# Taking a turned softmax block to its place through DRAM instead of by small transfers inside the chip

## The chip, the cores and the metric

The kernel runs on one core of one Trainium2 chip. The metric is the device time of one execution in microseconds (us), as the median of several executions. Profiled executions give the rows that are shown; their times are read from the start of the profiled span.

## The reference, cut to what matters

```python
B, H, S, Ns, D = (8, 8, 512, 32, 64)          # x: B,H,S,D   state: B,H,Ns,D
scores  = softmax(scale * x @ state.T)        # over the 32 states
xread   = scores @ state
scores2 = softmax(scale * state @ x.T)        # over the 512 rows of x: the state softmax
sread   = scores2 @ x
z = concatenate([xread, sread], axis=2)       # B,H,544,64 -> 4352 rows of 512
h = z @ w_in                                  # 512 -> 2048
out = (h * tanh(softplus(h))) @ w_out         # 2048 -> 512
```

All of it is float32. The change touches only the way from `scores2` to `sread`.

## The kernel before, in words

The eight batches are worked off one after another. `state @ w_in` is formed for each batch and head first (tiles `swp`, split into a rounded high part `swh` and a rest `swl`), so that the first large product (tiles `ph`, function `gemm1`) runs straight from the attention weights `ah` and `al`, the high part and the rest of `at`. Mish turns `ph` into `gu`, sums of its parts (`sums`) and their high and low parts (`gh`, `gl`) feed the second large product (tiles `acc`, function `products`), whose results leave through `o`. After the `xread` rows of all batches come the `sread` rows of all of them (key "s").

The attention of batch b+1 is spread over the steps of batch b. For batches 3 to 7 the function `pieces` gives its vector work in small portions, and a table says at which step each comes. The order there is: `e1` (the scores turned, their maximum, the difference), both exponentials, `soft2_t` (lines 376 to 389, which the change rewrites), the sums and the division of `e1`, then `at` (`e1` turned back), `ah` by ScalarE and `al` by VectorE. TensorE reads the result of `soft2_t`, the tile `e2T`, in `sread`, at the head of the visit `sw0` of the batch (step 6 of the batch before); the same visit forms the batch's first `swp`, and ScalarE and VectorE make `swh` and `swl` from it.

Two things order this work. TensorE's instructions have the order in which they are written from start to end, and VectorE's and ScalarE's too, but for a stretch after the first batch (while `dve.on` and `act.on` are false, about 90 to 158 us), where a planner that simulates the engines puts them in order. SyncE's queue, which issues almost all transfers, is ordered by that planner throughout. A helper at line 93 records the engines' instructions, so nearly all rows name line 93.

Buffers matter too. The tiles `e1`, `e2b` (named `turned` in the code) and `at` share a tag with two buffers. `at` is made from `e1`, so it takes the buffer of `e2b`, and has to wait until nothing reads `e2b` any more:

```python
def temp(name):
    return pool.tile([P, 2, S], F32, tag="t", name=name)     # pool has bufs=2
```

`e2T` lies in the only buffer of the tag "sc", where the exponentials of the scores were. For the first batch both have places in another tile, and its transfers show in the profile as `scs<-e2b`.

Of the kernel before, what the change touches and what calls it, by code (L numbers as in the profile page):

```python
# [9 lines left out]
F32 = mybir.dt.float32  # L10
# [7 lines left out]
P = 128  # L18
B, H, S, NS, D = 8, 8, 512, 32, 64
DM, DF = 512, 2048  # L20
T = S + NS
NC = H // 2
NT = S // P
# [77 lines left out]
def state_attention_mish_kernel(ctx, tc, x_turned, x, state_wide, state, w_in, w_out, out):  # L101

    nc = tc.nc
# [22 lines left out]
    def temp(name):  # L126
        return pool.tile([P, 2, S], F32, tag="t", name=name)
# [8 lines left out]
    dram = ctx.enter_context(tc.tile_pool(name="dram", bufs=1, space=bass.MemoryType.DRAM))  # L136
# [192 lines left out]
    def flat2(a):  # L329
        return a.rearrange("p u s -> p (u s)")  # L330
# [4 lines left out]
    def attention(b):  # L335
# [26 lines left out]
        soft = {}  # L362
# [13 lines left out]
        def soft2_t():  # L376
            dve.tensor_scalar_add(soft["sm"], soft["sm"], 1e-9)
            dve.reciprocal(soft["rs"], soft["sm"])
            turned = flat2(temp(f"e2b_{b}"))
            dve.transpose(  # L380
                turned.rearrange("p (s q n) -> p q s n", s=4, q=8),
                soft["sc"].rearrange("p u (g s t) -> p (u g) s t", s=4, g=4))
            place = soft.pop("e2T") if b == 0 else pool.tile([P, 2, S], F32, tag="sc", name=f"e2T_{b}", bufs=1)
            e2T = soft["e2T"] = flat2(place).rearrange("p (c u t n) -> p c u t n", c=NC, u=2, t=NT)
            for c in range(NC):
                for s in range(4):
                    nc.sync.dma_start(  # L387
                        e2T[s * NS:(s + 1) * NS, c].rearrange("t u g n -> t (u g n)"),
                        turned[c * NS:(c + 1) * NS, s * 2 * P:(s + 1) * 2 * P])

        def soft1_t():
            e1 = soft["e1"] = temp(f"e1_{b}")
# [37 lines left out]
        def softs():  # L430
            whole(soft1_t())
            soft2_m()
            soft1_x()
            with behind("exp"):
                soft2_x()
            whole(soft1_n())
            soft2_t()

        def pieces():
# [14 lines left out]
            with behind("exp"):  # L454
                soft2_x()
            yield
            soft2_t()
            yield
            dve.tensor_reduce(sums, g, AX.X, ALU.add)
# [29 lines left out]
        def alone(step):  # L489
            return lambda _: step()  # L490

        return dict(
            sc=lambda _: scores(second_bank if b == 0 else first_bank if b > 3 else misc), tr=alone(soft1_t), em=alone(soft2_m), ex=alone(soft1_x),
            ee=alone(soft2_x), no=alone(soft1_n), pr=alone(soft1_a), tl=alone(soft2_t), sr=sread, read=read, aT=aT, softs=softs, pieces=pieces, last=lambda: whole(soft1_a()))

    srds = {}
# [101 lines left out]
    def split_g(key, g):  # L598
        gh, gl = high_g(key, g)
        low_g(g, gh, gl)  # L600
        return gh, gl
# [13 lines left out]
    def gemm1(b, j, aT, sw):  # L615

        phs = [ps_h.tile([P, 512], F32, tag="ph", name=f"ph_{b}_{j}_{k}") for k in two]
        order = [(side, k, n) for side in two for k in two for n in (0, 1, 2, 3, 4, 5)]
        if b == 1:
            order = [(side, k, n) for k in two for n in (0, 1, 3, 4, 2, 5) for side in two]  # L620
        for side, k, n in order:
            kc, which = divmod(n, 3)
            left = sw[j][which // 2][:, kc, k * P:(k + 1) * P]
            right = aT[kc][which % 2][:, side * 256:(side + 1) * 256]
            pe.matmul(
                phs[k][:, side * 256:(side + 1) * 256], left, right,
                start=(n == 0 and side == 0), stop=(n == 5), skip_group_check=True)
        return phs
# [24 lines left out]
    def mish(b, j, phs):  # L653
        g = new_g(f"{b}_{j}")
        for k, ph in enumerate(phs):
            take_g(g, k, ph)
        return g
# [263 lines left out]
    for j in range(SLOTS):  # L921
        g = split_g(f"{key}_{j}", mish(key, j, gemm1(key, j, aTs[key], sw)))
# [73 lines left out]
    for k in range(-LAG, len(steps)):  # L996
# [64 lines left out]
        key, j, p = steps[k]  # L1061
# [49 lines left out]
```

## Time and profile before

| what | value |
|---|---|
| time, median of 3 runs | 619.66 us (619.39 to 619.7) |
| time of the profiled execution | 619.45 us |
| its span | 617.6 us (1.85 us lie around it) |
| TensorE, busy | 608.5 us, 6006 products |
| VectorE, busy | 487.0 us |
| ScalarE, busy | 358.6 us |
| granted TensorE clock | 1.00 of full speed in nearly all of the span |
| transfers | 81.75 MB, mean 132 GB/s |

PE is TensorE, PEld its weight loads, DVE is VectorE, ACT ScalarE, SPq the queue of SyncE that issues transfers. Products are pipelined, so that a short gap between the starts of two of them does not show as idle time.

### The profile page before, as it was taken

The page shows a single profiled execution, that of the slowest core. Times are in us where ns is not written, and L with a number is a line of the kernel's source. Part 1 is how long each engine was busy: PE and PEld are TensorE (multiplying, and loading weights), DVE is VectorE, ACT ScalarE, POOL GpSimd, SP SyncE. Part 2 cuts the span into 40 slices and gives each one's busy share as a digit, 9 for nine tenths or more (in the row PEclk, how much of TensorE's full clock was granted, in tenths as well). Part 3 has the DMA queues.
Part 4 walks back from the last instruction along what each step waited for, and adds up shares of the span by engine and source line. Part 5 has one row for each costly group of instructions (what it writes and reads, how often), then busy time and mean ns, then how long its engine had stood idle before and what let it go on. Part 6 is the DMA issues. An engine that isn't in the chain of part 4 may idle for free.

```text
span 617.6 us, 14712 instructions
## 1 busy us (share of the span) xinstructions
PE 608.5 (99%) x6006; PEld 552.9 (90%) x6006; DVE 487.0 (79%) x1085; ACT 358.6 (58%) x716; POOL 0.7 (0%) x6
## 2 busy tenths in 40 slices
PE   7999999999999999999999999999999999999997
PEld 5777688888889999998999989999999899999997
DVE  5989899976778678779787878779787776768586
ACT  4999794335457555655547554755557454554542
POOL 0000000000000000000000000000000000000000
PEclk9999999999999999999999999999999999999999
DMA  8959722511451434314403422314422230203301
GB/s 322 419 201 370 256 106 78 197 71 32 147 211 72 147 147 171 138 35 171 172 26 128 152 94 117 138 40 167 172 89 75 79 136 2 103 1 115 126 35 35
DMA packets 23202, 81.75 MB, mean 132 GB/s; under 512 B 3936, under 2 KB 8416, under 8 KB 18272
## 3 DMA queue, kind: packets, MB, share of 16 engines
q1 hardware_dynamic: 22848, 80.56, 36.0%
q8 instruction: 47, 0.77, 0.5%
q10 hardware_dynamic: 288, 0.26, 0.1%
q14 instruction: 19, 0.16, 0.1%
HBM read 63.50 MB, written 13.11 MB: 124 GB/s over the span
## 4 chain that ended last, share of the span: by engine, by line
PE 69%; DVE 11%; ACT 10%; SPq 4%; issue 4%; DMA 1%; DVEq 0%; ACTq 0%
PE acc L93 36%; PE ph L93 20%; PE swp L93 4%; SPq L387 4%; PE ph_s L93 4%; PE acc_s L93 3%; ACT L93 3%; DVE gl L93 2%; PE sc L93 2%; ACT gh L93 2%; DVE swl L93 2%; DVE o L93 1%; ACT swh L93 1%; ACT wir L93 1%; DVE sums L93 1%
## 5 line engine op out<-in xcount | busy, mean ns | idle before, releaser
L93 PE MATMUL acc<-wo,gh 128*128 128x256 f32 (+1 forms) x1024 | 224.1, 308 | 0.6 <-DVE o L93 0.3
L93 PEld LDWEIGHTS acc<-wo,gh 128*128 128x128 f32 x1024 | 162.0, 188 | 21.5 <-issue 9.1
L93 PE MATMUL acc<-wo,gl 128*128 128x256 f32 (+1 forms) x512 | 155.9, 305 | 0.0
L93 PE MATMUL ph<-ah,swh 128*128 128x256 f32 (+1 forms) x484 | 130.1, 287 | 0.5 <-DVE swl L93 0.2
L93 PE MATMUL ph<-al,swh 128*128 128x256 f32 (+1 forms) x484 | 128.7, 284 | 0.0
L93 PE MATMUL ph<-ah,swl 128*128 128x256 f32 (+1 forms) x484 | 127.1, 285 | 0.2
L93 PE MATMUL acc<-wt,gh 128*128 128x256 f32 x576 | 107.8, 277 | 0.5 <-DVE o L93 0.2
L93 PEld LDWEIGHTS acc<-wo,gl 128*128 128x128 f32 x512 | 96.1, 188 | 5.3
L93 PEld LDWEIGHTS ph<-ah,swh 128*128 128x128 f32 x484 | 88.4, 188 | 5.9 <-ACT gh L93 1.2
L93 ACT CAST gh<-sums 128x512 fp32r<-128x512 f32 x96 | 59.9, 624 | 52.1 <-DVE sums L93 51.8
L93 PEld LDWEIGHTS ph<-al,swh 128*128 128x128 f32 x484 | 88.2, 188 | 1.4 <-DVE al L93 0.2
L93 PEld LDWEIGHTS ph<-ah,swl 128*128 128x128 f32 x484 | 87.2, 188 | 2.6 <-DVE swl L93 1.3
L93 PEld LDWEIGHTS acc<-wt,gh 128*128 128x128 f32 x576 | 86.7, 188 | 1.2 <-issue 1.2
L93 DVE TENSOR_TENSOR gl<-gu,gh 128x384 fp32r<-128x384 f32 x96 | 53.0, 552 | 36.2 <-ACT gh L93 35.6
L93 ACT ACTIVATE gu<-ph 128x256 f32<-128x256 f32 x192 | 61.2, 385 | 33.1 <-PE ph L93 32.9
L93 PE MATMUL acc<-wt,gl 128*128 128x256 f32 x288 | 79.5, 276 | 0.0
L93 ACT CAST gh<-gu 128x384 fp32r<-128x384 f32 x96 | 49.7, 517 | 49.5 <-PE acc L93 48.9
L93 DVE TENSOR_TENSOR gl<-sums,gh 128x512 fp32r<-128x512 f32 x96 | 66.1, 689 | 4.4 <-ACT gh L93 4.4
L93 DVE TENSOR_TENSOR swl<-swp,swh 128x512 fp32r<-128x512 f32 (+1 forms) x82 | 42.8, 567 | 24.8 <-ACT swh L93 24.5
L93 PEld LDWEIGHTS acc<-wt,gl 128*128 128x128 f32 x288 | 54.1, 188 | 0.0
L93 DVE TENSOR_TENSOR sums<-gu 128x128 f32<-128x128 f32 x192 | 46.3, 282 | 7.1 <-ACT gu L93 7.1
L93 ACT CAST swh<-swp 128x512 fp32r<-128x512 f32 (+1 forms) x82 | 35.5, 503 | 23.5 <-PE swp L93 23.4
(103 smaller groups left out, 737.6 us busy)
## 6 DMA issues: line engine op xcount, KB each, us to landing
w_in<-w_in_kept SPq DMA_DIRECT2D x10, 1536.0 KB, 7.2
w_in<-w_in_kept SPq DMA_DIRECT2D x9, 1024.0 KB, 5.1
wir<-in_w_in_dram SPq DMA_DIRECT2D x16, 512.0 KB, 9.1
wor<-in_w_out_dram SPq DMA_DIRECT2D x16, 512.0 KB, 9.3
x<-in_x_dram SPq DMA_DIRECT2D x8, 1024.0 KB, 5.0
out_dram<-o SPq DMA_DIRECT2D x32, 256.0 KB, 2.3
xT<-in_x_turned_dram SPq DMA_DIRECT2D x7, 1024.0 KB, 6.3
w_in_kept<-w_in SPq DMA_DIRECT2D x8, 512.0 KB, 10.7
```

The source lines that it names most:

```text
L93: made = method(*args, **kwargs)
L387: nc.sync.dma_start(e2T[s * NS:(s + 1) * NS, c].rearrange("t u g n -> t (u g n)"), turned[c * NS:(c + 1) * NS, s * 2 * P:(s + 1) * 2 * P])
```

## The change

Each of the eight state softmaxes ends in a block of 128 partitions by 4 KB (`turned`) that has to be laid out anew over the partitions. Before, sixteen transfers of 32 partitions by 1 KB take it from SBUF to SBUF, all issued by SyncE. After, one transfer writes the block to a DRAM tile of its own (512 KB for each batch), and four transfers read it back, each filling 32 partitions with four runs of 1 KB. The reads wait for the write to land. What is computed stays the same; the buffers in SBUF stay the same.

```diff
             place = soft.pop("e2T") if b == 0 else pool.tile([P, 2, S], F32, tag="sc", name=f"e2T_{b}", bufs=1)
-            e2T = soft["e2T"] = flat2(place).rearrange("p (c u t n) -> p c u t n", c=NC, u=2, t=NT)
-            for c in range(NC):
-                for s in range(4):
-                    nc.sync.dma_start(
-                        e2T[s * NS:(s + 1) * NS, c].rearrange("t u g n -> t (u g n)"),
-                        turned[c * NS:(c + 1) * NS, s * 2 * P:(s + 1) * 2 * P])
+            place_of = flat2(place)
+            soft["e2T"] = place_of.rearrange("p (c u t n) -> p c u t n", c=NC, u=2, t=NT)
+            kept_e2 = dram.tile([P, 4 * 2 * P], F32, name=f"e2_kept_{b}")
+            nc.sync.dma_start(kept_e2, turned)
+            for s in range(4):
+                nc.sync.dma_start(
+                    place_of[s * NS:(s + 1) * NS].rearrange("t (c x) -> t c x", c=NC),
+                    kept_e2[:, s * 2 * P:(s + 1) * 2 * P].rearrange("(c t) x -> t c x", c=NC))
```

## Rows read from the trace of the kernel before

**Rows 1.** The page: busy time by engine, and the chain by engine.
```profile
PE 608.5 (99%) x6006; PEld 552.9 (90%) x6006; DVE 487.0 (79%) x1085; ACT 358.6 (58%) x716; POOL 0.7 (0%) x6
...
PE 69%; DVE 11%; ACT 10%; SPq 4%; issue 4%; DMA 1%; DVEq 0%; ACTq 0%
```

**Rows 2.** Waits, whole span: waiting engine and tile, releaser, us in total, times, longest.
```profile
DVE at L93 <- DMA e2T<-e2b: 13.5, 5, 3.7
...
DVE at L93 <- issue: 2.4, 1, 2.4
...
PEld acc L93 <- DVE o L93: 1.4, 4, 0.4
...
PEld ph L93 <- DVE swl L93: 1.3, 6, 0.3
```

**Rows 3.** Timeline of SP, 332 to 359 us: start, duration, line, transfer, count.
```profile
334.01 10.03 SPq L387 DMA_DIRECT2D e2T<-e2b  x16
348.20 0.35 SPq L154 DMA_DIRECT2D xT<-in_x_turned_dram  x1
```

**Rows 4.** Timeline of VectorE, 332 to 359 us (attention of batch 5).
```profile
345.55 1.25 DVE L93 STREAM_TRANSPOSE at<-e 128x1024 f32<-128x1024 f32 x1 [2.21 <-DMA e2T<-e2b]
...
350.38 1.22 DVE L93 TENSOR_TENSOR al<-at,ah 128x1024 fp32r<-128x1024 f32 x1
351.52 1.95 DVE L93 TENSOR_TENSOR swl<-swp,swh 128x256 fp32r<-128x256 f32 x4
```

**Rows 5.** Timeline of TensorE where it first reads e2T, batches 3 to 7.
```profile
212.47 0.26 PE L93 MATMUL swp<-x,e2T 128*32 128x64 f32 x4
...
278.83 0.26 PE L93 MATMUL swp<-x,e2T 128*32 128x64 f32 x4
...
347.03 0.26 PE L93 MATMUL swp<-x,e2T 128*32 128x64 f32 x4
...
414.53 0.26 PE L93 MATMUL swp<-x,e2T 128*32 128x64 f32 x4
...
482.13 0.26 PE L93 MATMUL swp<-x,e2T 128*32 128x64 f32 x4
```

**Rows 6.** Timeline of TensorE: the same product of acc after visits 3 and 7.
```profile
222.54 0.28 PE L93 MATMUL acc<-wo,gh 128*128 128x256 f32 x1
...
494.27 0.38 PE L93 MATMUL acc<-wo,gh 128*128 128x256 f32 x1
```

**Rows 7.** Timeline of ScalarE: swh in the visits of batches 3, 5 and 7.
```profile
215.12 1.63 ACT L93 CAST swh<-swp 128x256 fp32r<-128x256 f32 x4 [2.92 <-PE swp L93]
...
349.68 1.63 ACT L93 CAST swh<-swp 128x256 fp32r<-128x256 f32 x4 [0.87 <-PE swp L93]
...
484.84 1.61 ACT L93 CAST swh<-swp 128x256 fp32r<-128x256 f32 x4
```

**Rows 8.** Timeline of VectorE, 196 to 222 us (batch 3).
```profile
206.44 1.25 DVE L93 STREAM_TRANSPOSE at<-e 128x1024 f32<-128x1024 f32 x1 [1.27 <-DMA e2T<-e2b]
...
215.52 2.06 DVE L93 TENSOR_TENSOR swl<-swp,swh 128x256 fp32r<-128x256 f32 x4 [0.54 <-ACT swh L93]
```

**Rows 9.** Timeline of VectorE, 467 to 495 us (batch 7).
```profile
481.68 1.25 DVE L93 STREAM_TRANSPOSE at<-e 128x1024 f32<-128x1024 f32 x1 [3.24 <-DMA e2T<-e2b]
...
487.64 1.95 DVE L93 TENSOR_TENSOR swl<-swp,swh 128x256 fp32r<-128x256 f32 x4
```

**Rows 10.** Transfers by line: count, KB each, median us from issue to landing.
```profile
out_dram<-o SPq DMA_DIRECT2D x32, 256.0 KB, 2.3
...
w_in_kept<-w_in SPq DMA_DIRECT2D x8, 512.0 KB, 10.7
...
e2T<-e2b SPq DMA_DIRECT2D x112, 32.0 KB, 1.9
```

**Rows 11.** Timeline of VectorE, 150 to 156 us (batch 2).
```profile
155.25 1.25 DVE L93 STREAM_TRANSPOSE at<-e 128x1024 f32<-128x1024 f32 x1 [3.75 <-DMA e2T<-e2b]
```

## The prediction

> **What bounds the kernel now.** I read the page first. TensorE is busy for 99% of the span and holds 69% of the chain that ended last [rows 1]. By that share alone nothing could be won outside TensorE. But the products are pipelined, so the share hides gaps between their starts, and the same chain gives 11% to VectorE, 10% to ScalarE and 4% to SyncE's queue. So I went on to the waits, to see who is late for TensorE. VectorE's transposition into `at` stands still behind transfers from `e2b` to `e2T` for 13.5 us in five cases, and for 2.4 us in one more that the view calls issue [rows 2]: six softmaxes, batches 2 to 7. The weight loads of `ph` wait for `swl`, those of `acc` for `o`, 1.3 and 1.4 us [rows 2]; both are VectorE's work, and both come shortly after `at`.
>
> The third view is SyncE's timeline beside VectorE's, for batch 5. The sixteen issues begin at 334.01 and last 10.03 us [rows 3], so the queue needs about 0.63 us for each; the last lands about 344 to 345. `at` starts at 345.55 after 2.21 us of idleness [rows 4]: VectorE was ready at 343.34. `al` follows at 350.38, `swl` at 351.52 [rows 4].
>
> The fourth is TensorE's timeline, and it prices what this lateness costs. The first product that reads `e2T` comes once in every batch. Its starts [rows 5] give the length of four batches: 212.47 to 278.83 is 66.36 us, then 68.20, 67.50 and 67.60. The work is the same in each. The first of these batches starts with the visit of batch 3, where `at` was transposed six microseconds ahead of the visit [rows 8] and nothing waits; the others start with visits 4, 5 and 6, where `at` is late. So the late visits cost 1.84, 1.14 and 1.24 us, 4.22 in all. Visit 7 has no next one to measure to, so I go from the visit's first product to the same product of `acc`: 222.54 less 212.47 is 10.07 us in visit 3, and 494.27 less 482.13 is 12.14 us in visit 7 [rows 5, 6], 2.07 us more. TensorE loses 6.3 us in these four places, and this is the ceiling of what an earlier `at` can give back there.
>
> **The change part by part.** *Removed: sixteen issues of 0.63 us in each of eight softmaxes.* They are on SyncE's queue, which has nothing else ready in the late visits: the next issue after them is that of `xT` at 348.20 [rows 3]. In themselves they are worth nothing; what they hold is `e2b`'s buffer.
>
> *Added: one write of 512 KB.* No row shows this transfer alone. Nearest below is the store of 256 KB to DRAM, 2.3 us to landing; above are eight writes of the same size to DRAM at 10.7 us [rows 10]. Those eight were issued together: 4 MB in 10.7 us, by which 256 KB more are worth some 0.7 us. I take 2.3 + 0.7 = 3.0 us, an estimate from these two rows, because here the write goes alone, as the stores do. Both ends are kept for the range. The write lands at about 334.0 + 3.0 = 337.0. Only it reads `e2b`, so the buffer is free six microseconds before VectorE comes for it at 343.34. Anything up to 9.3 us would do.
>
> *Added: four reads of 128 KB that wait on SyncE for the write.* Behind that wait stand only the reads themselves and, at 348.20, `xT`. I price an issue at 0.63 us as now, and the landing between 1.9 us (32 KB) and 2.3 us (256 KB) [rows 10]; I take 2.3, since a read has four times the bytes of the transfer that it replaces. Three issues ahead of the last and its landing are 1.9 + 2.3 = 4.2 us. `e2T` is whole 3.0 + 4.2 = 7.2 us after 334.0, at 341.2. TensorE wants it at 347.03 [rows 5], 13.0 us after the start; so 5.8 us are to spare, and the DRAM detour is hidden under the products of the running batch. Were that cover gone, it would cost its whole 7.2 us in each visit.
>
> One rule speaks against the detour. The Trainium skill's page "DMA: Bandwidth & Descriptors", section "Anatomy of one DMA — SWDGE (gpsimd) path", puts most of a transfer's fixed 2 us down to the receipt of the last write and says that the delay can be surprisingly long when the target is HBM. By its fit the write would take 3.2 us (2.0 and 512 KB at 436 GB/s), an estimate, and the chain 7.4 us instead of 7.2. The stores to DRAM in [rows 10] show no such long delay, and the sum stays as it is.
>
> *Moved: the end of `at`'s wait.* In visit 5 `at` starts 2.21 us earlier, and `al` with it. Next `swl` meets its other source, `swh`, which waits for TensorE's `swp` and does not move: 349.68 [rows 7]. In visit 3 `swl` begins 0.40 us after `swh` (215.52 and 215.12) [rows 7, 8]. The same distance puts `swl` of visit 5 at 350.08 instead of 351.52: 1.44 us earlier, against a loss there of 1.14. In visit 7, with 3.24 us of wait [rows 9], `swl` goes from 487.64 to 485.24 [rows 7, 9], 2.40 us against 2.07. The other two stand between these, in the same order of work. Each time the shift exceeds the loss by about 0.3 us, so all of the loss should go, and visit 3 shows that the sequence behind (the rest, `gl`, `o`) then keeps TensorE waiting no longer. In batches 2 and 3, waits of 3.75 and 1.27 us end too [rows 8, 11]; I take no gain there, since batch 3's visit loses nothing, and for batch 2, in the freely ordered stretch, I have no row of TensorE that waits for it.
>
> *Sum.* 6.3 us less. The profiled execution took 619.45 us; 619.45 - 6.3 = 613.15. The median of the runs is 0.21 us higher, so 613.4 us is forecast, 1.0% faster.
>
> **The rivals.**
>
> *Part of it is taken back (about 616 us).* The planner knows other transfer times and may order VectorE, ScalarE and SyncE anew in the stretch where it is free, where three of the eight softmaxes lie, the waiting `at` of batch 2 among them [rows 11]. VectorE is busy for 79% of the span [rows 1], so a late piece of its work can't always be made up; I put a worse order there at 1 to 3 us, about one to two losses like those of the late visits. Or `al` or `o` still come late and only some of the 6.3 is won. For it: margins of only 0.3 us. Against it: visit 3 runs without loss in the same order. 619.66 - 6.3 + 2.5 = 615.9.
>
> *Nothing moves (619.5 us).* TensorE's gaps could have other causes, such as the results `o`, which VectorE draws from `acc` itself, so that the wait for `at` only fills time. A page's rule bears on the opposite view: the Trainium skill's "Perfetto Trace Analysis", section "Identifying the Most-Contended Engine", calls busy time of matmuls a bad measure, because they are pipelined; that agrees with gaps that 99% hides, and the starts of [rows 5] show them. Against this rival: the loss follows the wait from visit to visit (2.21 us lose 1.14, 3.24 lose 2.07, and the 1.27 of batch 3, long before its visit, lose none).
>
> *Slower (about 623 us).* The write lands like the writes of `w_in_kept`, in 10.7 us [rows 10]. Then `e2T` is whole 10.7 + 4.2 = 14.9 us after the start, and with a slower issue 15.4; TensorE waits up to 2.4 us in each of the four visits, 9.6 us, while the old loss of 6.3 goes because VectorE has that time too: 619.66 - 6.3 + 9.6 = 623.0. The visit suffers from a landing above 13.0 - 4.2 = 8.8 us, and the total is slower than before from about 8.8 + 6.3/4 = 10.4 us. For it: only the row of 10.7, and that each read waits for the write. Against it: those eight went at once, and in the late visits the queue is otherwise empty.
>
> **How the numbers follow.** All of the 6.3 us: chance 0.66, its own range 612.4 to 614.6 (0.8 us more, should the free stretch gain as well, to 1.2 less). Part of it: 0.17. Nothing: 0.06. Slower: 0.11. The range 612.4 to 617.0 takes in the first and most of the second. A measurement here tells a change from 0.2%, 1.2 us. Faster by more than that: 0.66 and nearly all of 0.17, and I say 0.82; within: 0.07; slower: 0.11.
>
> **What would show it.** After the change the waits name no transfer ahead of `at`; SyncE's row has one write and four reads in some 7 us; `e2T`'s last read lands about 5 us before its first product; the starts of that product stand 66.4 us apart from batch to batch, four times; `swl` begins 0.4 us after `swh`. The prediction is wrong if `at` has a new releaser, if the weight loads of `swp` wait for reads from DRAM, if the distances stay above 67 us, or if the stretch from 90 to 212 us has grown.

## The result, and the profile after

The changed kernel takes 612.13 us (median of its runs, 611.85 to 612.28) against 619.66 us. The ratio is 0.9879, with the interval 0.9867 to 0.9891: 7.5 us less, 1.2% faster. The forecast was 613.4 us, with a range of 612.4 to 617.0. The direction and the mechanism came as forecast; the time lies 0.27 us below the low end of the range.

The page of the kernel after: busy time by engine, the chain by engine, and the span. They answer to [rows 1].

```profile
span 610.1 us, 14552 instructions
...
PE 601.8 (99%) x6006; PEld 550.4 (90%) x6006; DVE 487.1 (80%) x1085; ACT 359.1 (59%) x716; POOL 0.7 (0%) x6
...
PE 82%; DVE 7%; ACT 6%; DMA 2%; issue 2%; SPq 1%; DVEq 0%; ACTq 0%
```

No share of busy time moved by more than a point, although the span is 7.5 us shorter. What moved is the chain: TensorE holds 82% of it instead of 69%, VectorE 7% instead of 11%, ScalarE 6% instead of 10%, SyncE's queue 1% instead of 4%. TensorE's busy time fell by 6.7 us with the same 6006 products at the same granted clock (1.000 in both). So the busy time before held some 6.7 us in which products waited, and the share of 99% hid them.

Timelines after around the visit of batch 5: SyncE's queue, then VectorE, then ScalarE, then VectorE and ScalarE in the visit of batch 7. They answer to [rows 3, 4, 7, 9].

```profile
331.05 0.33 SPq L387 DMA_DIRECT2D e_kept<-e2b  x1
334.19 1.74 SPq L389 DMA_DIRECT2D e2T<-e_kept  x4
345.30 0.35 SPq L154 DMA_DIRECT2D xT<-in_x_turned_dram  x1
...
340.34 1.24 DVE L93 STREAM_TRANSPOSE at<-e 128x1024 f32<-128x1024 f32 x1
...
347.19 2.06 DVE L93 TENSOR_TENSOR swl<-swp,swh 128x256 fp32r<-128x256 f32 x4 [0.53 <-ACT swh L93]
...
346.79 1.63 ACT L93 CAST swh<-swp 128x256 fp32r<-128x256 f32 x4 [2.92 <-PE swp L93]
...
479.82 2.06 DVE L93 TENSOR_TENSOR swl<-swp,swh 128x256 fp32r<-128x256 f32 x4 [0.53 <-ACT swh L93]
...
479.42 1.63 ACT L93 CAST swh<-swp 128x256 fp32r<-128x256 f32 x4 [2.92 <-PE swp L93]
```

Five issues take the place of sixteen. The write starts at 331.05, and the reads, which wait for it, begin 3.1 us later: in this batch the write took 3.1 us to land. `at` starts at 340.34, 9.3 us after the start, with nothing in brackets behind it: VectorE comes to it without a pause. `swl` now has ScalarE's `swh` as its releaser and begins 0.40 us after it, in visit 5 and in visit 7 alike. That is the distance that only visit 3 had before.

TensorE's timeline after: the first product that reads `e2T`, batches 3 to 7, and the product of `acc` behind visit 7. They answer to [rows 5, 6].

```profile
211.51 0.31 PE L93 MATMUL swp<-x,e2T 128*32 128x64 f32 x6
...
277.81 0.30 PE L93 MATMUL swp<-x,e2T 128*32 128x64 f32 x5
...
344.14 0.26 PE L93 MATMUL swp<-x,e2T 128*32 128x64 f32 x4
...
410.45 0.26 PE L93 MATMUL swp<-x,e2T 128*32 128x64 f32 x4
...
476.77 0.26 PE L93 MATMUL swp<-x,e2T 128*32 128x64 f32 x4
...
486.85 0.28 PE L93 MATMUL acc<-wo,gh 128*128 128x256 f32 x1
```

The distances are 66.30, 66.33, 66.31 and 66.32 us, where before they were 66.36, 68.20, 67.50 and 67.60. From the first product of visit 7 to the one of `acc` it is 10.08 us instead of 12.14. All batches now have the length of the one that had lost nothing.

The DMA issues after: count, size of each, median us from issue to landing. They answer to [rows 10].

```profile
out_dram<-o SPq DMA_DIRECT2D x32, 256.0 KB, 2.2
...
w_in_kept<-w_in SPq DMA_DIRECT2D x8, 512.0 KB, 11.0
...
e_kept<-e2b SPq DMA_DIRECT2D x8, 512.0 KB, 2.6
...
e2T<-e_kept SPq DMA_DIRECT2D x28, 128.0 KB, 2.9
```

A write of 512 KB that goes alone lands in 2.6 us (the median of eight, which took 2.6 to 3.2 us), a quarter of the 11.0 us of `w_in_kept`. Those eight were issued within 6.6 us, the first lands 9.0 us after its issue and the others about 1.2 us apart, so that by these figures most of the 11.0 us is the wait for transfers ahead.

**Where the 7.5 us came from.** I cut the span at three products of TensorE that both kernels have: a product of `acc` at 91 us, which lies ahead of the first changed transfer, then the first read of `e2T` by batch 3, then a product of `acc` shortly behind visit 7, at 494.49 us before and 486.96 us after. Each kernel was profiled three times in all (the further ones are e9, e10 and e8, e11 below).

| stretch, us | before, three profiles | after, three profiles | first pair |
|---|---|---|---|
| start to 91 us | 91.55, 91.17, 91.19 | 91.02, 90.79, 91.20 | 0.53 |
| to the visit of batch 3 | 120.92, 120.87, 120.89 | 120.49, 120.49, 120.47 | 0.43 |
| visits 3 to 7 | 282.02, 281.52, 282.02 | 275.45, 275.42, 275.39 | 6.57 |

The rest behind them is the same within 0.1 us. The middle row is a gain of 0.4 us that repeats to within a few hundredths. The first row lies ahead of the change: up to its first transfer, at 92 us, every engine does the same work in the same order in both kernels, the 47 issues of SyncE among it. This row scatters by 0.4 us within either kernel, and over the profiles of all thirteen runs, which are alike up to there, it lies between 90.70 and 92.10 us.

### The profile page after: what moved, and what is told of

Read it like the earlier page. It is cut to its first block, busy times and chain, and to the rows that moved or that the text cites. A ratio compares the mean times of both kernels' runs of the same rounds, so it can differ in the third digit from the quotient of the medians.

```text
span 610.1 us, 14552 instructions
## 1 busy us (share of the span) xinstructions
PE 601.8 (99%) x6006; PEld 550.4 (90%) x6006; DVE 487.1 (80%) x1085; ACT 359.1 (59%) x716; POOL 0.7 (0%) x6
## 4 chain that ended last, share of the span: by engine, by line
PE 82%; DVE 7%; ACT 6%; DMA 2%; issue 2%; SPq 1%; DVEq 0%; ACTq 0%
PE acc L93 45%; PE ph L93 24%; PE swp L93 5%; PE ph_s L93 4%; PE acc_s L93 3%; ACT L93 2%; ACT wir L93 1%; PE sc L93 1%; DMA wir<-in_w_in_dram 1%; ACT wor L93 1%; DVE gu_w L93 1%; ACT g L93 1%; DVE swl L93 1%; DVE gu_t L93 1%; DVE wt L93 1%
```

## The experiments

The theory: the time was lost because sixteen slow issues held the buffer of `e2b`, so that `at`, and with it `al` and `swl`, came late in visits 4 to 7. Rivals: the earlier `e2T` is worth something by itself; fewer issues on SyncE's queue are; the planner's other order of the free stretch is; and, against the theory's reading of the margins, a slow way through DRAM would cost little or much.

**e1: one write, sixteen reads.** The write frees the buffer; the queue keeps as many issues as before.

```diff
             nc.sync.dma_start(kept_e2, turned)
-            for s in range(4):
-                nc.sync.dma_start(place_of[...], kept_e2[...])
+            for c in range(NC):
+                for s in range(4):
+                    nc.sync.dma_start(
+                        soft["e2T"][s * NS:(s + 1) * NS, c].rearrange("t u g n -> t (u g n)"),
+                        kept_e2[c * NS:(c + 1) * NS, s * 2 * P:(s + 1) * 2 * P])
```

> One write of the block to DRAM as after the change, then sixteen reads of 32 KB back, in the place of four. SyncE issues as much as before the change (17 issues in each softmax) and the tile e2T is whole as late as before it (an estimate from rows: 2.6 us for the write, sixteen issues of 0.43 us, 2.4 us for the last landing, 11.9 us after the start, where before took 11.9 too), but the buffer of e2b is free after 2.6 us. Theory (the buffer is what counts): the late visits keep their gain of 6.6 us, and a few tenths are lost where TensorE waits for sixteen transfers in place of four: 612.3 to 613.5 us. First rival (the load of SyncE's queue counts): 619 to 620 us. Second rival (the early arrival of e2T counts): 619 us or more.

Measured: 613.49 us (613.31 to 613.69), ratio 0.9909 (0.9895 to 0.9922) to 619.51 us beside it. Timelines of SyncE's queue and VectorE, batch 5:

```profile
332.92 0.33 SPq L387 DMA_DIRECT2D e_kept<-e2b  x1
335.55 7.29 SPq L390 DMA_DIRECT2D e2T<-e_kept  x16
...
342.21 1.24 DVE L93 STREAM_TRANSPOSE at<-e 128x1024 f32<-128x1024 f32 x1
```

`at` starts without a pause although the sixteenth read is issued at 342.84, after `at` has begun. All five visits take 10.07 to 10.08 us. So neither the number of issues nor an early `e2T` made the gain of the late visits: how long transfers *read the buffer* did. The time is at the upper end of the range given for it. The 1.4 us more than after are mainly lost in the free stretch, which is 1.25 us longer (121.74 us against 120.49; before had 120.92); there the products of batch 0 that read `e2T` last 1.86 us after 0.71 us of idleness, against 1.10 us and 0.05 in the kernel after.

**e2 and e3: the change in batches 3 to 7 alone, and in batches 0 to 2 alone.**

```diff
+            if b > 2:                  # e3: if b < 3
                 nc.sync.dma_start(kept_e2, turned)
                 ...
+            else:
+                ...                    # the sixteen transfers of before
```

> The change for batches 3 to 7 alone; batches 0 to 2 keep their sixteen transfers. Theory: the late visits give all of their 6.6 us and the rest of the gain, some 0.4 us between 90 and 160 us, is missing: 612.5 us. Rival (the planner's new order in the free stretch makes a good part of the gain): 614 to 616 us.

> The change for batches 0 to 2 alone; batches 3 to 7 keep their sixteen transfers. Theory: 0.3 to 0.4 us less than before, where TensorE's reads of e2T no longer stop at one wait after another: 619.2 to 619.4 us. Rival (the planner's new order): 616 to 618 us. If the half microsecond that the changed kernel gained ahead of 22 us belongs to the change and not to chance, it should show here too: 618.7 us.

Measured: e2 612.50 us (612.00 to 612.96), ratio 0.9892 (0.9879 to 0.9906); e3 620.08 us (619.15 to 621.10), ratio 1.0013 (1.0004 to 1.0022). The late batches carry the gain. That e2 came out at the very number that was given for it is luck: its free stretch lost 0.65 us where nothing was to change (121.57 us against 120.92), and the start of its profile was the quickest of all (90.70 us). e3 is a miss: it should have gained a little and came out 0.6 us slower. In its profile (619.43 us, one of its quicker executions) the free stretch is 0.4 us shorter, as in the kernel after, and the late visits lose some 0.2 us more than in the first profile of before, so that the two cancel; why its median lies above before's was not found. Nor can 0.4 us in the free stretch be counted as sure for any edit: e2 leaves that stretch's transfers as they were, does the same operations in the same order there, and is still longer in it; why was not found.

**e4: the sixteen transfers of before on two queues, without DRAM.** If it is the hold that counts, halving it without any detour must do as well.

```diff
-                    nc.sync.dma_start(
+                    (nc.sync if s < 2 else nc.gpsimd).dma_start(
                         e2T[s * NS:(s + 1) * NS, c].rearrange("t u g n -> t (u g n)"),
                         turned[c * NS:(c + 1) * NS, s * 2 * P:(s + 1) * 2 * P])
```

> The kernel before, with eight of the sixteen transfers inside the chip issued by SyncE and eight by GpSimd, so no DRAM. The buffer of e2b is held for about 5 us of issues and 2 us of landing (an estimate: eight issues of 0.63 us), under the 9.3 us that VectorE leaves. Theory: the whole gain of the late visits without any DRAM, about 613 us. Rival (the load of SyncE's queue counts): half of it, about 616 us. Rival (something in the way through DRAM counts, such as fewer but larger transfers): 619 us.

Measured: 612.63 us (611.88 to 613.19), ratio 0.9894 (0.9880 to 0.9908). Timelines of SyncE's queue, GpSimd and VectorE, batch 5:

```profile
332.33 4.97 SPq L387 DMA_DIRECT2D e2T<-e2b  x8
...
332.88 3.93 POOL L387 DMA_DIRECT2D e2T<-e2b  x8 [62.12 <-DVE sums L93]
...
341.57 1.24 DVE L93 STREAM_TRANSPOSE at<-e 128x1024 f32<-128x1024 f32 x1
```

All sixteen are issued in 5.0 us, `at` does not wait, the five visits take 10.07 us each, and the time is that of the DRAM way within the scatter. DRAM is one means of shortening the hold, and not the only one.

**e5 and e6: the changed kernel with the buffer held longer.** Dummy copies of `e2b` to DRAM, written in the program behind the four reads, keep the buffer in use; SyncE issues five of them while it waits for the write. `e2T` arrives about as early as in the kernel after (7.7 us after the start in e6's batch 5, 7.3 there).

```diff
+            if b > 2:
+                junk = dram.tile([P, 4 * 2 * P], F32, name=f"junk_{b}")
+                for i in range(8):     # e6: 16
+                    c, s = i // 4 % 4, i % 4
+                    nc.sync.dma_start(
+                        junk[c * NS:(c + 1) * NS, s * 2 * P:(s + 1) * 2 * P],
+                        turned[c * NS:(c + 1) * NS, s * 2 * P:(s + 1) * 2 * P])
```

> The changed kernel; for batches 3 to 7 SyncE also copies eight pieces of e2b (32 KB each) to a DRAM tile that nobody reads, five of them while it waits for the write and three behind the four reads. e2T comes as early as in the changed kernel; e2b is held longer: 0.33 us, 2.3 us, four reads of 0.45 and three copies of 0.45, 1.7 us of landing, about 7.5 us after the start, under the 9.3 us at which VectorE comes for the buffer. Theory: nothing is lost, 612.1 to 612.6 us. Rival (the load of the queue or the extra traffic counts): 613.5 to 615 us.

> The same with sixteen copies, eleven of them behind the reads, so that e2b is held about 11.2 us, as long as before the change, while e2T still comes some 7 us after the start. Theory (the buffer of e2b counts): VectorE waits some 1.9 us for the buffer again and the late visits lose most of their 6.6 us again: 617 to 619.5 us. Rival (the early arrival of e2T counts): 612.1 to 612.6 us.

Measured: e5 612.03 us (611.29 to 612.51), ratio 0.9878 (0.9863 to 0.9892) to 619.68 us; e6 620.77 us (618.15 to 621.81), ratio 1.0014 (1.0001 to 1.0028). Timelines of e6, SyncE's queue and VectorE, batch 5:

```profile
334.15 0.33 SPq L387 DMA_DIRECT2D e_kept<-e2b  x1
334.53 2.83 SPq L396 DMA_DIRECT2D junk<-e2b  x5
337.47 1.78 SPq L389 DMA_DIRECT2D e2T<-e_kept  x4
339.30 5.40 SPq L396 DMA_DIRECT2D junk<-e2b  x11
...
345.91 1.25 DVE L93 STREAM_TRANSPOSE at<-e 128x1024 f32<-128x1024 f32 x1 [2.38 <-DMA junk<-e2b]
```

The reads are issued by 339.25, so `e2T` is there in good time, and still the whole gain is gone: `at` waits 2.38 us for dummy copies that nobody needs, and starts 11.76 us after the transfers began (11.54 in before [rows 3, 4]). The batches after visit 3 are again longer, 69.27, 67.63 and 68.06 us, and visit 7 takes 12.16: a loss of 8.1 us over the 66.32 and 10.08 of the kernel after. The time lies 1.3 us above the range that was given for it; the wait was put at 1.9 us and came as 2.4 to 4.0 in the four late visits, so the losses were larger than those of before. In e5 the last dummy is issued 6.6 us after the start, `at` starts at 340.59, 9.30 us after it, without a pause, and nothing is lost. This pair settles the theory: what counts is when the buffer comes free, and a longer hold costs nothing as long as it ends before VectorE comes for the buffer. All profiles agree. From the first read of `e2T` by batch 3 to the product behind visit 7 it is 275.39 to 275.45 us in the kernel after, e1, e2, e4 and e5, whose last transfer out of `e2b` in batch 5 lands at most 8.4 us after the start; it is 281.5 to 283.6 us in the kernel before, e3 and e6, where it lands after 11.3 to 11.7 us. VectorE comes at about 9.3 us.

**e7: the reads late.** Twenty-four copies of a constant stand between the write and the reads on SyncE's queue, kept in this order. The buffer is free early, `e2T` comes late. It puts a price on the rival that ends slower.

```diff
-            nc.sync.dma_start(kept_e2, turned)
+            sp = InOrder(tc, nc.sync)
+            sp.dma_start(kept_e2, turned)
+            if b > 2:
+                junk = dram.tile([24, NS, 2 * P], F32, name=f"junk_{b}")
+                for i in range(24):
+                    c = i % 4
+                    sp.dma_start(junk[i], bds[c * NS:(c + 1) * NS].rearrange("p b c n -> p (b c n)")[:, :2 * P])
             for s in range(4):
-                nc.sync.dma_start(
+                sp.dma_start(
```

> The changed kernel; for batches 3 to 7 SyncE makes 24 copies of a constant (32 KB each) to DRAM between the write and the four reads, so that e2b is free after 2.6 us but e2T is whole only after about 15.2 us (0.33, 24 issues of 0.46, four of 0.45, 2.4 us of landing), 2.1 us after TensorE comes for it. It prices the rival of the prediction that ends slower: TensorE waits about 2.1 us in each of four visits, 8.4 us: 620.5 us. If TensorE had more cover than the 13.1 us that I count: 612.1 to 613 us.

Measured: 643.00 us (642.18 to 644.10), ratio 1.0385 (1.0366 to 1.0403). The direction is right, the price far too low. In batch 5 `e2T` is whole 16.8 us after the start instead of 15.2, since the 24 copies take 0.51 us each and not 0.46. Timelines of e7, SyncE's queue and TensorE, batch 5:

```profile
344.32 0.33 SPq L93 DMA_DIRECT2D e_kept<-e2b  x1
344.69 12.14 SPq L93 DMA_DIRECT2D junk<-bds  x24
356.93 1.78 SPq L93 DMA_DIRECT2D e2T<-e_kept  x4
...
361.22 1.31 PE L93 MATMUL swp<-x,e2T 128*32 128x64 f32 x64 [3.71 <-DMA e2T<-e_kept]
```

Windows of e7 (stretch, its length, then the busy time of TensorE, its weight loads, VectorE, ScalarE and GpSimd with counts, the granted TensorE clock, DMA share, GB/s), first behind the stops of batch 3, then around that of batch 5:

```profile
216.00:220.00 4.00, 3.85 (x53) 2.38 (x54) 0.56 (x2) 0.96 (x3) 0.00 (x0) 0.50 0.60 225
...
356.00:361.00 5.00, 1.51 (x14) 1.31 (x12) 3.25 (x7) 1.04 (x2) 0.00 (x0) 1.00 0.41 130
361.00:364.00 3.00, 2.78 (x96) 1.99 (x104) 0.00 (x0) 0.00 (x0) 0.00 (x0) 0.66 0.35 49
364.00:368.00 4.00, 4.00 (x47) 3.02 (x32) 2.22 (x6) 2.57 (x7) 0.00 (x0) 0.83 0.87 338
368.00:372.00 4.00, 4.00 (x38) 4.00 (x37) 3.83 (x13) 0.99 (x3) 0.00 (x0) 1.00 0.39 160
```

TensorE stands still for 3.71 us, and behind the stop it is granted 0.66 and then 0.83 of full speed, a mixture of its two levels (0.50 is 1.2 GHz, 1.00 is 2.4 GHz); in batch 3, behind two stops with 1.10 us of products between them, it ran for 4 us at 0.50. The visits take 11.45 to 12.35 us instead of 10.07; that of batch 3 takes 15.72, because there the second stop, 2.79 us long, falls inside the visit and waits for `w_in`, which SyncE's queue loads too. The batches between stand 71.7 to 72.8 us apart (76.6 behind batch 3). In visits 4 to 7 a stop costs 5.3 to 6.8 us: 3.7 to 4.8 us of idle time, and 1.4 to 2.3 us by which the visit behind it is longer, in the stretch where the granted clock is lower. That the clock is the whole of this second part is not shown.

**e8 to e11: both kernels once more, unchanged,** to tell the change's work from chance at the start of the span.

> The changed kernel once more, on the chip of these runs. Theory: 6.6 us in the late visits and 0.36 us in the free stretch, so 6.9 to 7.0 us less than before; what the first comparison showed beyond that (7.5 us) lies ahead of 22 us, where neither kernel has done anything different yet, and is chance. Rival (the changed program also starts faster): 7.5 us again, and its profile is half a microsecond ahead of before at 22 us again.

> The kernel before once more, for its profile: is the half microsecond that the changed kernel's profiles show ahead of 22 us chance? Theory (chance): the first product of acc after 22 us starts up to 0.7 us earlier or later than in the first profile of before, and the time is within 618.5 to 620 us. Rival (the changed program starts faster): it starts within 0.15 us of the first profile.

> The same, a third profile of the kernel before: the spread of the three starts at 22 us is the size of chance there.

> A third profile of the changed kernel on the same chip. Theory: its start at 22 us lies in the spread of the three starts of before, its five reads of e2T stand 66.3 us apart and its stretch from 91 to 160 us is 0.3 to 0.5 us shorter than that of before. Rival: it starts half a microsecond ahead of all three.

Measured: e8 (after) 611.69 us (611.43 to 612.37), ratio 0.9875 (0.9860 to 0.9890) to 619.68 us, 8.0 us less where 6.9 to 7.0 were expected, a miss; one execution each of e9 and e10 (before) 618.51 and 619.13 us, with a third one beside them 618.25 us; e11 (after) 611.97 us, 6.3 to 7.2 us below these three. Their profiles gave the table above. The product at 91 us comes at 91.17 and 91.19 in the two further profiles of before and at 91.20 in the last of after; behind 22 us the first product of `acc` starts at 24.98, 24.57 and 24.65 us before and at 24.38, 24.29 and 24.66 after. So the 0.53 us of the first pair at the start are within the scatter of equal work. But the medians give 7.5 and 8.0 us where the table's two other rows give 7.0 in the first pair, so that chance as the whole of the rest is likely and not shown.

## Why the prediction was right, and where its number was not

**The mechanism held in the late visits.** The write landed in 2.6 us in the median and in 3.1 in batch 5 (3.0 forecast). In batch 5 the last read is issued by 335.93 and lands at 338.35, so `e2T` is whole 7.3 us after the start (7.2). That these two agree so well is luck: an issue was put at 0.63 us and took 0.44, and a read's landing was put at 2.3 us and took 2.9, outside the bounds of 1.9 and 2.3 that the prediction gave it. TensorE wants it at 344.14, 13.1 us after the start, which leaves 5.8 us (5.8). `at` starts 9.3 us after the start (9.3) and waits for no transfer. `swl` begins 0.40 us behind `swh`, and the distances of 66.4 us came as 66.3. The rule of the Trainium skill that spoke against the detour ("DMA: Bandwidth & Descriptors", section "Anatomy of one DMA — SWDGE (gpsimd) path", a receipt that can be surprisingly long when the target is HBM) does not show here: the row says 2.6 us, less than the 3.2 us of its fit, which only the slowest of the eight writes reached.

**The rivals.** *Nothing moves* fell: TensorE's gaps went with the wait. *Part taken back* did not happen; the free stretch became 0.4 us shorter, not longer. Yet it is no empty rival: e1, which is ordered differently there, lost 0.8 us in that stretch against before. (e2's 0.65 us can't be put down to this, for its order is that of before.) *Slower* had the right place and the wrong price. It reckoned 2.4 us for each visit, as idle time alone; e7 shows 5.3 to 6.8 us when TensorE stands for 3.7 to 4.8 us, and the granted clock falls behind each stop.

**The step that failed is the term that was put at nothing: "I take no gain there", said of batches 2 and 3, for want of a row of TensorE that waits for `at`.** In batch 2 TensorE does not wait for `at`, it waits for `e2T` itself, and this arrival was never compared with the first product that reads it there. The runs showed 0.43 us in the free stretch in its place. This alone does not carry the time out of the range; against the forecast, 1.27 us more were saved, and they are three things:

- *0.43 us in the free stretch*, taken as zero. Three profiles of either kernel agree (0.38 to 0.45). TensorE's timelines show where, in the `sread` products of batches 0 and 2, which the prediction did not read. Before, with SyncE's issues for batch 2:

```profile
105.93 1.38 PE L93 MATMUL srp<-x,scs 128*32 128x64 f32 x64
...
154.75 1.47 PE L93 MATMUL srp<-x,e2T 128*32 128x64 f32 x64
...
143.78 10.01 SPq L387 DMA_DIRECT2D e2T<-e2b  x16
```

  and after:

```profile
105.49 1.10 PE L93 MATMUL srp<-x,scs 128*32 128x64 f32 x64
...
154.17 1.10 PE L93 MATMUL srp<-x,e2T 128*32 128x64 f32 x64
...
143.15 0.32 SPq L387 DMA_DIRECT2D e_kept<-e2b  x1
145.78 1.74 SPq L389 DMA_DIRECT2D e2T<-e_kept  x4
```

  The same 64 products take 1.10 us instead of 1.38 and 1.47. Of what batch 0 gains nothing is left by 122 us (the same product of `ph` starts 30.32 us behind the product at 91 us in both kernels), so the 0.43 us are in the main the 0.37 of batch 2. There the reason can be read: before, SyncE issues the sixteen transfers from 143.78 on for 10.01 us, and the last lands at 155.03, when the products have begun at 154.75; after, the reads are issued by 147.52 and the last lands at 150.28. The other runs agree: where the last transfer lands behind the first of these products, they take 1.36 to 1.50 us (e1, e2 and the two further profiles of before), and 1.10 in all the rest. Batch 0's transfers had landed 2.0 us ahead of its products; that these were held up by waits for sixteen transfers, one behind the other, is argued and not shown.
- *0.27 us in the late visits*: 6.57 instead of 6.3. By the forecast's own distances it is 6.46, for the batch of visit 3, which served as the measure of one without loss, was itself 0.06 us too long, which makes the losses of the next three too small by 0.03 to 0.05 us each. The last 0.11 us lie behind the product to which visit 7 was measured.
- *0.53 us at the start*, ahead of anything that the change does. The further profiles show that equal work scatters by more than that there; as said under e8, chance as its whole cause is likely and not shown. Without it the time would lie inside the range: 613.4 less 0.43 and 0.27 is 612.7.

The remaining 0.04 us are rounding of the forecast. Each of these is small; but the low end was only 1.0 us below the forecast (0.8 us, the most that the free stretch was given, taken off the profiled 613.15 and not off 613.4), and three small terms of the same sign had no room in it. The size of the late term, for which I had measured rows, was right to 4%; the term that I set to zero for want of a row was the one that failed.

**What stays open.** Why e3 is 0.6 us slower than before, why e2's free stretch is longer, which waits made the products of batch 0 longer, and whether the 0.5 to 1.0 us by which the medians exceed the profiles' 7.0 us are all chance. A kernel in which `e2b` has a buffer of its own, the most direct way to take the wait away, was not tried.

## What to carry to other kernels

When an engine waits for a buffer, look at how long the last reader holds it, and not only at how fast the data arrive: in batch 5 sixteen issues of 0.63 us held it for 11.3 us, one write for 3.1 us, and the detour of 7.3 us through DRAM was free since TensorE came for its end 5.8 us later. Price such a wait by the distance between the starts of a product that comes once in each repetition (66.3 against 67.5 to 68.2 us); a busy share of 99% shows nothing of it. Before an edit's gain elsewhere is set to zero, look at every consumer of what it moves, in every place where it acts (here of `e2T` and not of `at` alone), and leave the range room for the scatter between runs, here 1.4 us over thirteen profiles in the first 91 us alone.

## What the runs showed of the hardware

- The granted TensorE clock fell to its lower level in e7 behind stops, and stayed there for some microseconds: 0.66 of full speed in the 3 us that follow a stop of 3.71 us, 0.50 in the 4 us that follow stops of 0.85 and 2.79 us. The mean over the span was 0.981 there, and 0.999 or 1.000 in all other profiles.
- The price of an issue on SyncE's queue depends on the transfer. 32 KB from SBUF to SBUF in 32 rows: 10.03 us for sixteen, 0.63 each; the same 32 KB from DRAM: 7.29 for sixteen, 0.46 each; 128 KB from DRAM: 1.74 for four, 0.44 each; one of 512 KB to DRAM: 0.33. GpSimd's queue issued eight of the 32 KB transfers in 3.93 us, 0.49 each, beside SyncE's eight in 4.97.
- A write of 512 KB to DRAM landed in 2.6 us alone (median of eight, 2.6 to 3.2) and in 11.0 us as one of eight issued within 6.6 us.
